# An opening list planned with other step lengths on TensorE, and idle matrix products placed only in that list's gaps

## The chip, the cores and the metric

One core of one Trainium2 chip. The metric is the device time of one execution in microseconds (us), lower is better; comparisons use the median of several executions.

## The reference

Attention in two parts over 8 batches, 8 heads, 576 positions and 64 dimensions, summed, and then a normalised gated feed-forward layer over the 4608 tokens. Cut to what matters:

```python
# coarse part: q, k, v averaged over groups of 4 positions, 144 x 144 softmax, repeated 4 times
out_up = np.repeat(sm_attn(q_d, k_d, v_d), 4, axis=2)
# local part: every position sees the positions at a distance under 4
mask = np.abs(pos[:, None] - pos[None, :]) < 4
scores = np.where(mask, 0.125 * np.matmul(q, k.transpose(0, 1, 3, 2)), -1e9)
out_local = np.matmul(softmax(scores), v)
x = (out_up + out_local)            # 4608 tokens x 512
xn = x / np.sqrt(np.mean(x * x, -1, keepdims=True) + 1e-6) * rms_g
g = xn @ w_gate                     # 512 -> 1536
return (g / (1 + np.exp(-g)) * (xn @ w_val)) @ w_out
```

The weights come as 64-bit numbers; the kernel takes two 32-bit words of each and makes a high and a low part of it.

## The kernel before, in words

The tokens are worked in 18 chunks of 256. For a chunk the local attention makes x, x is normalised and turned (`turn`, TensorE transposes into PSUM), split into `xh` (ScalarE) and `xl` (VectorE, line 304), and the feed-forward layer (`Forward`) runs over 12 slices f of the hidden width: `first` (two groups of 12 products into one `ps_h` buffer, gate and value), `tanh` on ScalarE, `gate` and `product` on VectorE, `high` (ScalarE) and `low` (VectorE or GpSimd), and `second`, 6 products into `ps_o`, two slices later.

The start of the program is different, and all of the change lies in it. It makes at once: the sums of q, k, v over groups of 4 (`OpeningSums`); eight coarse pieces p0 to p7, one for each pair of heads of the first two batches (`Coarse`: `scores`, `peak`, `powers`, `turn`, `copy`, `values`, `scaled`, `store`); the local attention of chunks 0, 1 and 2 on TensorE (`Dense`, which I call c0, c1 and c2: `scores`, softmax, `flip`, `copy`, `values`, then `add_up` of the pieces for c0 and `add_rows` for c1 and c2); the decoding of 36 blocks of weights (`load_weight`: `fetch` on the SP queue, `scale`, `last_bits`, `join`, `high`, `split` on ScalarE and VectorE); and `Forward` of chunk 0. Every one of these steps is a task with an engine, a length in us, a due time, the tasks it comes after and the buffers it takes. `Plan.run` goes through them as a list scheduler: of the steps that can start first, on the engine that can start first, the one with the earliest due time is written out next. So the lengths in the `task(...)` calls set the order of the instructions on each engine; they have no other effect. The order is then fixed, and an engine that comes to a step too early waits there. What follows (chunks 1 to 17 of `Forward`, with the attention of the chunk after) is written out in loops and ordered without these lengths.

TensorE's clock is granted by a gate, in steps that the profile shows. To keep it up, the kernel writes idle products: matrix products of a bf16 unit matrix into an accumulator that the next step overwrites anyway. Before the change these are in `place`, which every `Coarse` step that takes an accumulator calls: two products of 224 columns each time.

PSUM has three `ps_h`, two `ps_o` and three `ps_a` accumulators; pieces p0, p2, p4, p6 use `ps_a`, the others `ps_h`. The raw weight blocks have eight places until their `join` is done.

Of the kernel before, what the change touches and what calls it, by code (L numbers as in the profile page):

```python
# [19 lines left out]
P = 128  # L20
B, H, S, D = 8, 8, 576, 64
FAC = 4
SD = S // FAC
# [4 lines left out]
DM, DF = H * D, 1536  # L28
# [13 lines left out]
FIRST = 1  # L42
WARM = 2
V_ROWS = 50.0
# [31 lines left out]
class Plan:  # L76
# [33 lines left out]

    def start(self):
        free = self.free = {e: 0.0 for e in ("PE", "ACT", "DVE", "POOL", "SP", "DMA", "PORT")}
# [16 lines left out]
    def run(self, until=1e9):  # L129
        free, ready = self.free, self.ready  # L130
        while self.left:
# [18 lines left out]
            s, e, t = best  # L150
            if s >= until:
                return
            cost = next(o for o in t.options if o[0] == e)[1]
            t.start = s
            free[e] = s + cost - OVERLAP.get(e, 0.0)
            if t.port and e in SHARING:
# [20 lines left out]
def attn_moe_kernel(  # L177
# [280 lines left out]
    def sums_of(b, hp):  # L458
        if (b, hp // 2) not in sums:
            sums[b, hp // 2] = Sums(b, hp // 2)  # L460
        return sums[b, hp // 2]

    class Coarse:

# [31 lines left out]
        def plan(self, at, after=()):  # L496
# [16 lines left out]
            for par in range(2):  # L513
                turn = task("PE", 0.55, lambda par=par: self.turn(par), at - TAIL, [exps[par]], allocs=[t[par]], uses=[a[par]])
                copies.append(task("ACT", 0.38, lambda par=par: self.copy(par), at, [turn], uses=[a[par], t[par]]))
            inv = task("DVE", 0.33, self.invert, at, exps, uses=[z])
            values = self.valued = task("PE", 1.3, self.values, at - TAIL, [*copies, *sm.ready_vs], allocs=[o], uses=[*a, sm.vs_buf])
            scaled = self.done = task("DVE", 0.42, self.scaled, at, [values, inv], allocs=[og], uses=[o, z])
# [24 lines left out]
        def place(self, n=2 * SD):  # L543
            if loose:
                return self.pool.tile([HALF, n], FP32, name=self.tag)
            t = self.pool.tile([P, DM], FP32, name=self.tag)
            for _ in range(WARM):
                nc.tensor.matmul(
                    out=t[:, 2 * SD:].rearrange("p (t c) -> p t c", t=2), lhsT=masks["ident"],
                    rhs=bcast(masks["ident"][:, :(DM - 2 * SD) // 2], 1, 2), start=True, stop=True, skip_group_check=True,  # L550
                )
            return t[:HALF, :n]
# [319 lines left out]
    class Dense:  # L872
# [8 lines left out]
        def plan(self, sums, pieces, mask, at, end):  # L881
# [14 lines left out]
            for par in range(2):  # L896
                sb = s_bufs[par] if early else s_bufs[0]
                made = self.plan_softmax(par, at, scores, made, sp[par], sb)
                t = made[0]
                tp = buf("ps_a")  # L900
                t = task("PE", 0.7, lambda par=par: self.flip(par), at, [t], allocs=[tp], uses=[sb, tp])
# [14 lines left out]
            for par in range(2):  # L916
                values.append(task(
                    "PE", 0.8, lambda par=par: self.values(par), end - 15 + par,
                    [copies[par], *v_ready, *values[-1:], *(first if early else [p.valued for p in pieces])],
                    allocs=[] if early or par else x_bufs, uses=[*x_bufs, *v_bufs, *s_bufs],  # L920
                ))
# [8 lines left out]
            else:  # L930
                end += 25.0
                t = task(
                    "ACT", 0.1, self.load_up, end - 12, [stored[p.b, p.hp] for p in pieces], allocs=[self.xh_buf],
                    uses=[self.xh_buf], lag=9.0,
                )
                ups = [task("PE", 1.6, self.add_rows, end - 12, [t, *values], uses=[self.xh_buf, *x_bufs])]
            self.valued = values[-1:]
# [9 lines left out]
            for b in range(2):  # L947
                xs, tps = x_ts[b], buf("ps_h" if early else "ps_a")
                norms = self.plan_norms(b, xs, x_bufs, root, end)
                turn = task(  # L950
                    "PE", 0.6, lambda b=b: self.turn(b), end - 7 - TAIL, [*norms, *self.turns],
                    allocs=[tps] + ([self.xh_buf, self.xl_buf][not early:] if b == 0 else []), uses=[xs, self.xh_buf, self.xl_buf],
# [60 lines left out]
        def plan_scores(self, sums, pieces, mask, at, late):  # L1013
# [78 lines left out]
        def scores(self, b):  # L1092
            if b == 0:
                self.s = [ps_h.tile([P, 2, 2, 2, D], FP32, name="ps_h") for _ in range(2)]
                for par in range(2):
                    nc.tensor.matmul(
# [159 lines left out]
        def turn(self, b):  # L1256
# [5 lines left out]
            pool, tag = (ps_a, "ps_a") if self.c else (ps_h, "ps_h")  # L1262
            tp = self.xp[b] = pool.tile([P, KT, P], FP32, name=tag)
            for k in range(KT):
                last = nc.tensor.transpose(out=tp[:, k], in_=self.xn[b][:, k * P:(k + 1) * P], identity=ident_sb).ins
# [17 lines left out]
    class Forward:  # L1283
# [136 lines left out]
    def decode(n):  # L1420
# [9 lines left out]
        bits = task(  # L1430
            (("ACT", 0.67, at), ("DVE", 0.6, at)), 0, lambda e: last_bits(e.lower()), at, [got], uses=[raw],
        )
# [4 lines left out]
        joined.append(join_)  # L1437
        hi = task((("ACT", 0.62, at), ("DVE", 0.35, at)), 0, lambda e: high(e.lower()), at, [join_, *own], uses=[w])
        whole[n] = task("DVE", 0.69, split, at, [hi], uses=[w], port=True)
# [71 lines left out]
    with tc.manual_schedule():  # L1511
        plan.run()
    loose.append(True)
    listed.append(opened.copied)

# [97 lines left out]
```

## Time and profile before

| | |
|---|---|
| three executions | 1088.72, 1087.98, 1086.74 us (median 1087.98) |
| profiled execution | 1088.73 us, its span 1087.0 us, mean granted TensorE clock 0.983 |
| TensorE busy | 1044.5 us, 96% of the span |
| VectorE, ScalarE, GpSimd busy | 887.4, 626.4, 168.0 us |
| chain that ended last | TensorE 81%, VectorE 9%, DMA 4%, ScalarE 3% |

The span is the time from the first to the last instruction; the remaining 1.73 us of the profiled execution lie around it. Times in rows of the profile are us from the start of the span, a lone "x8" counts instructions, and the bracket at a row's end is the idle time of the engine ahead of it and what ended it. Steps are recorded one by one, so the step of a row is told by its line: 534 `scores`, 548 idle products, 574 `turn`, 589 `values` of a piece, 1096 and 1110 `scores` of a Dense chunk, 1158 `flip`, 1181 `values` of a Dense chunk, 1193 `add_up`, 1265 `turn` of a Dense chunk, 1344 `first`, 1380 `second`.

### The profile page before, as it was taken

What the parts mean: (1) busy time and instruction counts of PE and PEld (TensorE: products, weight loads), DVE (VectorE), ACT (ScalarE), POOL (GpSimd) and SP (SyncE); (2) the same over time, 40 slices, a digit from 0 to 9 for tenths busy, and PEclk for the clock granted to TensorE, in tenths of its full rate; (3) what the DMA queues carried; (4) which work ended last, traced back from release to release, by engine and by line L of the source; (5) the groups of instructions that cost most, each with busy time, mean ns of one, the idle gap of its engine ahead of it and who ended that gap; (6) DMA issues with size and microseconds to landing.
All of it is one profiled execution on the core that took longest, in us unless ns stands there. A gap on an engine that the chain in (4) does not pass through costs nothing.

```text
span 1087.0 us, 23815 instructions
## 1 busy us (share of the span) xinstructions
PE 1044.5 (96%) x8804; PEld 958.7 (88%) x8804; DVE 887.4 (82%) x1988; ACT 626.4 (58%) x2308; POOL 168.0 (15%) x225
## 2 busy tenths in 40 slices
PE   4888899899999999999999999999999999999998
PEld 2667799689998999999999999999999999999997
DVE  5778859885979998989898898989899998986432
ACT  5588743843747483848384838384738383746222
POOL 3201300312121121212121212020202010111000
PEclk8888999999999999999999999999999999999999
DMA  8488842564362635353535353313132222210000
GB/s 264 135 277 309 223 116 75 116 160 83 91 130 63 134 94 118 85 119 87 126 81 123 77 129 81 97 41 106 43 105 61 82 86 65 84 40 21 1 21 20
DMA packets 72731, 113.28 MB, mean 104 GB/s; under 512 B 26006, under 2 KB 33958, under 8 KB 72614
## 3 DMA queue, kind: packets, MB, share of 16 engines
q1 hardware_dynamic: 46342, 91.64, 27.7%
q0 software_dynamic: 8768, 15.95, 9.4%
q10 hardware_dynamic: 17504, 4.16, 1.8%
q8 instruction: 69, 1.13, 0.4%
q14 instruction: 48, 0.39, 0.1%
HBM read 99.92 MB, written 11.80 MB: 103 GB/s over the span
## 4 chain that ended last, share of the span: by engine, by line
PE 81%; DVE 9%; DMA 4%; ACT 3%; issue 2%; SPq 0%; ACTq 0%; POOL 0%; DVEq 0%; POOLq 0%
PE ps_h L1344 48%; PE ps_o L1380 25%; PE ps_a L589 2%; DVE prod L711 1%; PE ps_a L534 1%; PE ps_a L861 1%; DMA qk<-in_qk_sum_dram 1%; PE ps_a L574 1%; DVE sc L715 1%; ACT a_g L565 1%; DMA vs<-in_v_sum_dram 1%; DVE sil L1355 1%; DVE x_t L784 1%; DVE sil L1360 1%; DMA wo<-in_qk_sum_dram 1%
## 5 line engine op out<-in xcount | busy, mean ns | idle before, releaser
L1380 PE MATMUL ps_o<-wo,hs 128*128 128x512 f32 x1296 | 336.0, 397 | 0.9 <-DVE hs L1369 0.9
L1344 PE MATMUL ps_h<-xh,wg 128*128 128x256 f32 x1728 | 314.3, 279 | 0.0
L1344 PE MATMUL ps_h<-xh,wv 128*128 128x256 f32 x1728 | 310.0, 277 | 0.0
L1344 PEld LDWEIGHTS ps_h<-xh,wg 128*128 128x128 f32 x1728 | 267.1, 190 | 5.9 <-issue 0.4
L1344 PEld LDWEIGHTS ps_h<-xh,wv 128*128 128x128 f32 x1728 | 263.8, 188 | 3.4 <-issue 0.2
L1380 PEld LDWEIGHTS ps_o<-wo,hs 128*128 128x128 f32 x1296 | 228.9, 188 | 39.0 <-DVE hs L1369 1.1
L758 ACT ACTIVATE prod<-kv,sc 128x64 f32<-128x64 f32 x960 | 247.8, 427 | 16.0 <-DVE sc L749 11.3
L1344 PE MATMUL ps_h<-xl,wg 128*128 128x256 f32 x864 | 243.2, 282 | 7.8 <-DVE sil L1360 5.5
L1344 PE MATMUL ps_h<-xl,wv 128*128 128x256 f32 x864 | 241.5, 279 | 3.8 <-DVE sil L1355 3.8
L1352 ACT ACTIVATE sil<-ps_h 128x256 f32<-128x256 f32 x216 | 83.5, 387 | 224.7 <-PE ps_h L1344 205.8
L1344 PEld LDWEIGHTS ps_h<-xl,wg 128*128 128x128 f32 x864 | 163.8, 190 | 14.6 <-DVE sil L1360 6.6
L1344 PEld LDWEIGHTS ps_h<-xl,wv 128*128 128x128 f32 x864 | 162.4, 188 | 8.6 <-DVE sil L1355 4.8
L1366 ACT ACTIVATE hs<-sil 128x256 fp32r<-128x256 f32 x216 | 90.0, 418 | 132.4 <-DVE sil L1360 108.9
L765 POOL TENSOR_TENSOR prod<-sc,kv 128x256 f32<-128x256 f32 x120 | 92.3, 808 | 402.8 <-DVE sc L749 175.5
L784 DVE TENSOR_REDUCE x_t<-prod 128x128 f32<-128x896 f32 x120 | 127.4, 1073 | 20.9 <-PE ps_a L861 14.2
L1355 DVE SCALAR_TENSOR_TENSOR sil<-sil,ps_h 128x256 f32<-128x256 f32 x216 | 89.5, 414 | 61.6 <-ACT sil L1352 56.3
L711 DVE TENSOR_TENSOR prod<-q_t,kv 128x896 f32<-128x896 f32 x120 | 129.7, 1083 | 1.4 <-DMA kv<-in_k_pad_dram 1.2
L715 DVE TENSOR_REDUCE sc<-prod 128x14 f32<-128x896 f32 x120 | 128.2, 1075 | 0.0
L1369 DVE TENSOR_TENSOR hs<-sil,hs 128x256 fp32r<-128x256 f32 x213 | 93.4, 439 | 33.2 <-ACT hs L1366 33.1
L1360 DVE SCALAR_TENSOR_TENSOR sil<-sil,ps_h 128x256 f32<-128x256 f32 x216 | 89.3, 414 | 5.9 <-PE ps_h L1344 4.5
L372 POOL DMA_DIRECT2D qk<-in_qk_sum_dram x36 | 32.4, 900 | 253.4 <-DMA qk<-in_qk_sum_dram 222.2
L765 DVE TENSOR_TENSOR prod<-sc,kv 128x128 f32<-128x128 f32 x120 | 53.6, 467 | 0.7
(187 smaller groups left out, 940.8 us busy)
## 6 DMA issues: line engine op xcount, KB each, us to landing
kv<-in_k_pad_dram SPq DMA_DIRECT2D x60, 320.0 KB
kv<-in_v_pad_dram SPq DMA_DIRECT2D x60, 320.0 KB
qk<-in_qk_sum_dram POOLq DMA_DIRECT2D x36, 288.0 KB, 5.0
q_t<-in_q_band_dram SPq DMA_DIRECT2D x60, 128.0 KB
out_dram<-o_sb SPq DMA_DIRECT2D x30, 256.0 KB
vs<-in_v_sum_dram POOLq DMA_DIRECT2D x36, 144.0 KB, 3.4
qk<-in_qk_sum_dram SPq DMA_DIRECT2D x12, 288.0 KB
wo<-in_qk_sum_dram SPq DMA_DIRECT2D x2, 1152.0 KB
```

Source lines behind the costliest of these rows:

```text
L711: nc.vector.tensor_tensor(out=pr, in0=bcast(q[:, s0:s0 + 2], 2, NO), in1=window(k, s0), op=ALU.mult)
L715: nc.vector.tensor_reduce(out=self.sc[:, j, par, s0:s0 + 2], in_=self.pr[i], axis=AX.X, op=ALU.add,)
L758: nc.scalar.activation(out=self.pr[i][:, o, s], in_=self.v[j, par][:, s0 + s + o], func=AF.Copy, scale=p[:, s, o:o + 1],)
L765: (nc.vector if engine == "DVE" else nc.gpsimd).tensor_tensor(out=self.pr[i][:, a:b], in0=bcast(p[:, :, a:b].rearrange("p s o -> p o s"), ...
L784: nc.vector.tensor_reduce(out=self.x[j][:, s0:s0 + 2, par], in_=pr.rearrange("p o s d -> p s d o"), axis=AX.X, op=ALU.add,)
L1344: last = nc.tensor.matmul(out=self.p[f][:, t], lhsT=wi(f)[:, 0, k], rhs=xi[:, k], start=(n == 0), stop=(n == 3 * KT - 1),).ins
L1352: nc.scalar.activation(out=self.sil[f], in_=self.p[f][:, 0], func=AF.Tanh, scale=0.5)
L1355: nc.vector.scalar_tensor_tensor(out=self.sil[f], in0=self.sil[f], scalar=1.0, in1=self.p[f][:, 0], op0=ALU.add, op1=ALU.mult,)
L1360: nc.vector.scalar_tensor_tensor(out=self.sil[f], in0=self.sil[f], scalar=0.5, in1=self.p[f][:, 1], op0=ALU.mult, op1=ALU.mult,)
L1366: nc.scalar.activation(out=self.hs[f][:, 0], in_=self.sil[f], func=AF.Copy)
L1369: (nc.gpsimd if engine == "POOL" else nc.vector).tensor_tensor(out=self.hs[f][:, 1], in0=self.sil[f], in1=self.hs[f][:, 0], op=ALU.subtract,)
L1380: last = nc.tensor.matmul(out=self.o[j], lhsT=lhs[:, cols], rhs=rhs(f)[:, 0], start=(f == 0 and i == 0), stop=(f == NF - 1 and i == 2),).ins
```

## The change

The lengths of TensorE's steps in the opening are set to others (and three of VectorE's), so the list comes out in another order. The scheduler notes, for each TensorE step, how long it finds TensorE idle ahead of it (`plan.idle`). Idle products are no longer written at each `place`: a new function `warm` writes one for each 0.2 us of that noted idle time, at most 24, and it is called by every step that takes a new accumulator, `Dense.scores`, `flip`, `turn` and `first` included. The noted time goes to zero once used, and each later TensorE step overwrites it, so idle time ahead of a step that takes no accumulator is not filled. An idle product now has 256 columns. Two orderings are added (the load of the coarse rows for c1 after c0's `turn`, c2's `flip` after c1's `values`); for c2's load of coarse rows, c1's `turn` takes the place of the stores.

```diff
-WARM = 2
+IDLE = 0.2
+MOST = 24
...
             t.start = s
+            if e == "PE":
+                self.idle = s - free[e]
             free[e] = s + cost - OVERLAP.get(e, 0.0)
...
+    def warm(t):
+        n, plan.idle = min(int(plan.idle / IDLE), MOST), 0.0
+        for _ in range(n):
+            nc.tensor.matmul(
+                out=t[:, :2 * P].rearrange("p (t c) -> p t c", t=2), lhsT=masks["ident"],
+                rhs=bcast(masks["ident"], 1, 2), start=True, stop=True, skip_group_check=True,
+            )
...
-                turn = task("PE", 0.55, lambda par=par: self.turn(par), at - TAIL, [exps[par]], allocs=[t[par]], uses=[a[par]])
+                turn = task("PE", 0.45, lambda par=par: self.turn(par), at - TAIL, [exps[par]], allocs=[t[par]], uses=[a[par]])
...
             t = self.pool.tile([P, DM], FP32, name=self.tag)
-            for _ in range(WARM):
-                nc.tensor.matmul(
-                    out=t[:, 2 * SD:].rearrange("p (t c) -> p t c", t=2), lhsT=masks["ident"],
-                    rhs=bcast(masks["ident"][:, :(DM - 2 * SD) // 2], 1, 2), start=True, stop=True, skip_group_check=True,
-                )
+            warm(t)
...
-                    "ACT", 0.1, self.load_up, end - 12, [stored[p.b, p.hp] for p in pieces], allocs=[self.xh_buf],
+                    "ACT", 0.1, self.load_up, end - 12, [*[stored[p.b, p.hp] for p in pieces], *atts[0].turns], allocs=[self.xh_buf],
...
-                    "PE", 1.2 if b == 0 else 0.7, lambda b=b: self.scores(b), at + 2 * b,
+                    "PE", 2.2 if b == 0 else 1.15, lambda b=b: self.scores(b), at + 2 * b,
...
-                t = task("PE", 1.1, lambda par=par: self.flip(par), late + 8, made, allocs=[tp], uses=[sb, tp])
+                t = task("PE", 1.1, lambda par=par: self.flip(par), late + 8, [*made, *atts[1].valued], allocs=[tp], uses=[sb, tp])
...
-            task("ACT", 0.1, self.load_up, late + 20, [stored[p.b, p.hp] for p in pieces], allocs=[self.xh_buf], lag=9.0)
+            task("ACT", 0.1, self.load_up, late + 20, atts[1].turns, allocs=[self.xh_buf], lag=9.0)
...
             tp = ps_a.tile([P, 4, 2, D], FP32, name="ps_a")
+            warm(tp.rearrange("p x a k -> p (x a k)"))
...
                 self.p[f] = ps_h.tile([P, 2, C], FP32, name="ps_h")
+                warm(self.p[f].rearrange("p t n -> p (t n)"))
```

Of the other lengths: `values` of a piece 1.3 to 1.1, `flip` and `values` of a Dense chunk 0.7 and 0.8 to 1.1, `add_rows` 1.6 to 1.9, `turn` of a Dense chunk 0.6 to 0.8, `last_bits` on VectorE 0.6 to 0.42, `high` on VectorE 0.35 to 0.41.

The idle products, counted in TensorE's list: 80 of 224 columns before, two at each of 40 places. After, 24 ahead of p0's `scores`, 10 ahead of p0's `turn`, 10 ahead of p1's `turn`, 1 and 14 ahead of the `scores` of c0 and c1, none from there to p6's `values` (about 24 to 68 us of the old timeline), then 5 ahead of those, 1 ahead of c2's first `flip`, 18 and 1 ahead of c0's two `turn` steps, 15 ahead of the first `first`, and 5 ahead of the fifth: 104 of 256 columns.

Three places show what else moved. The first is the SP queue, between the loads of c0's rows (line 1049) and the first weight blocks (line 258); line 606 stores a piece's result. Before:

```order
L1049 DMA kv<-in_v_sum_dram 64x1x512 x3
L606 DMA up<-o_g 72x4x64
L1049 DMA kv<-in_v_sum_dram 64x1x512 x2
L258 DMA wg_1_702<-in_w_gate_dram 128x1024
L258 DMA wg_1_702<-in_w_val_dram 128x1024
L258 DMA wg_1_715<-in_w_out_dram 128x1024
L258 DMA wg_1_715<-in_w_gate_dram 128x1024
L606 DMA up<-o_g 72x4x64
```

and now, with the same steps on lines 1057, 262 and 614:

```order
L1057 DMA kv<-in_v_sum_dram 64x1x512 x5
L262 DMA wg_1_684<-in_w_gate_dram 128x1024
L262 DMA wg_1_684<-in_w_val_dram 128x1024
L262 DMA wg_1_712<-in_w_out_dram 128x1024
L614 DMA up<-o_g 72x4x64
L262 DMA wg_1_712<-in_w_gate_dram 128x1024
```

The first three weight blocks and the last two row loads no longer stand behind the store of p2's result.

The second is TensorE around the `scores` of p5 (`ps_h<-xh`), which are the first row before:

```order
L534 MATMUL ps_h<-xh 72x144 x4
L548 LDWEIGHTS q_t
L548 MATMUL ps_a<-q_t 128x224
L548 LDWEIGHTS q_t
L548 MATMUL ps_a<-q_t 128x224
L589 MATMUL ps_a<-hs,a_g 72x64 x8
L1181 MATMUL ps_o<-kv,x_t 32x64 x32
L1193 MATMUL ps_o<-o_g,q_t 32x128 x4
```

and the third row now, where 1168 is `flip`, 1203 `add_up`, 546 `scores`, 582 `turn`, 1191 `values` of c0 and 597 `values` of a piece:

```order
L1168 MATMUL ps_a<-ident_sb,wo_1_455 64x64 x16
L1203 MATMUL ps_o<-o_g,q_t 32x128 x4
L546 MATMUL ps_h<-xh 72x144 x4
L582 MATMUL ps_a<-ident_sb,a_g 72x72 x8
L1191 MATMUL ps_o<-kv,x_t 32x64 x32
L597 MATMUL ps_a<-hs,a_g 72x64 x8
L582 MATMUL ps_h<-ident_sb,a_g 72x72 x8
L1203 MATMUL ps_o<-o_g,q_t 32x128 x4
```

The idle products are gone, p5's `scores` stand ahead of p4's `turn`, and c1's second `flip` stands ahead of p5's `scores` (before, both of c1's `flip` steps came after the `scores` of p6).

The third is VectorE at the end of c0's attention, from the normalisation of x (line 1252) to `xl` (line 304). Before:

```order
L1252 TENSOR_SCALAR x_t<-ps_o,rinv 128x256 x2
L279 SCALAR_TENSOR_TENSOR o_sb<-o_sb,wg_1_715 128x512 x2
L279 SCALAR_TENSOR_TENSOR o_sb<-o_sb,wv_1_771 128x512
L294 TENSOR_TENSOR wv_0_876<-o_sb,wv_0_875 128x4x128
L304 SCALAR_TENSOR_TENSOR xl<-ps_h,g_sb,xh 128x128 x8
```

and now, the same steps on lines 1262, 283 (`join`), 298 (`split`), 295 (`high`) and 308:

```order
L1262 TENSOR_SCALAR x_t<-ps_o,rinv 128x256 x2
L283 SCALAR_TENSOR_TENSOR o_sb<-o_sb,wg_1_712 128x512
L283 SCALAR_TENSOR_TENSOR o_sb<-o_sb,wv_1_769 128x512 x2
L298 TENSOR_TENSOR wo_0_922<-o_sb,wo_0_921 128x512
L295 CAST wv_0_878<-o_sb 128x4x128
L308 SCALAR_TENSOR_TENSOR xl<-ps_h,g_sb,xh 128x128 x4
L298 TENSOR_TENSOR wg_0_820<-o_sb,wg_0_819 128x4x128
L308 SCALAR_TENSOR_TENSOR xl<-ps_h,g_sb,xh 128x128 x4
```

One more decoding step stands ahead of the first half of `xl`, and one between its halves. In ScalarE's list a `high` stands likewise between the halves of `xh`. Counted from the start to VectorE's first step of c0's normalisation, the list now holds 10 `join`, 10 `split` and 6 `last_bits` (before 10, 9 and 4); to ScalarE's first `squares`, 11 `scale`, 8 `high` and 5 `last_bits` (before 10, 7 and 6).

After the opening the instructions are the same, apart from buffer numbers; in the chunks that follow it at once some steps stand a few products earlier or later.

More of the change, by code (lines that the diff above doesn't have):

```diff
@@ L111, in start @@
     def start(self):
+        self.idle = 0.0
         free = self.free = {e: 0.0 for e in ("PE", "ACT", "DVE", "POOL", "SP", "DMA", "PORT")}
@@ L513, in plan @@
             for par in range(2):
-                turn = task("PE", 0.55, lambda par=par: self.turn(par), at - TAIL, [exps[par]], allocs=[t[par]], uses=[a[par]])
+                turn = task("PE", 0.45, lambda par=par: self.turn(par), at - TAIL, [exps[par]], allocs=[t[par]], uses=[a[par]])
                 copies.append(task("ACT", 0.38, lambda par=par: self.copy(par), at, [turn], uses=[a[par], t[par]]))
             inv = task("DVE", 0.33, self.invert, at, exps, uses=[z])
-            values = self.valued = task("PE", 1.3, self.values, at - TAIL, [*copies, *sm.ready_vs], allocs=[o], uses=[*a, sm.vs_buf])
+            values = self.valued = task("PE", 1.1, self.values, at - TAIL, [*copies, *sm.ready_vs], allocs=[o], uses=[*a, sm.vs_buf])
             scaled = self.done = task("DVE", 0.42, self.scaled, at, [values, inv], allocs=[og], uses=[o, z])
@@ L900, in plan @@
                 tp = buf("ps_a")
-                t = task("PE", 0.7, lambda par=par: self.flip(par), at, [t], allocs=[tp], uses=[sb, tp])
+                t = task("PE", 1.1, lambda par=par: self.flip(par), at, [t], allocs=[tp], uses=[sb, tp])
                 t = task(
@@ L917, in plan @@
                 values.append(task(
-                    "PE", 0.8, lambda par=par: self.values(par), end - 15 + par,
+                    "PE", 1.1, lambda par=par: self.values(par), end - 15 + par,
                     [copies[par], *v_ready, *values[-1:], *(first if early else [p.valued for p in pieces])],
@@ L932, in plan @@
                 t = task(
-                    "ACT", 0.1, self.load_up, end - 12, [stored[p.b, p.hp] for p in pieces], allocs=[self.xh_buf],
+                    "ACT", 0.1, self.load_up, end - 12, [*[stored[p.b, p.hp] for p in pieces], *atts[0].turns], allocs=[self.xh_buf],
                     uses=[self.xh_buf], lag=9.0,
                 )
-                ups = [task("PE", 1.6, self.add_rows, end - 12, [t, *values], uses=[self.xh_buf, *x_bufs])]
+                ups = [task("PE", 1.9, self.add_rows, end - 12, [t, *values], uses=[self.xh_buf, *x_bufs])]
             self.valued = values[-1:]
@@ L950, in plan @@
                 turn = task(
-                    "PE", 0.6, lambda b=b: self.turn(b), end - 7 - TAIL, [*norms, *self.turns],
+                    "PE", 0.8, lambda b=b: self.turn(b), end - 7 - TAIL, [*norms, *self.turns],
                     allocs=[tps] + ([self.xh_buf, self.xl_buf][not early:] if b == 0 else []), uses=[xs, self.xh_buf, self.xl_buf],
@@ L1094, in scores @@
                 self.s = [ps_h.tile([P, 2, 2, 2, D], FP32, name="ps_h") for _ in range(2)]
+                warm(self.s[0].rearrange("p b t a k -> p (b t a k)"))
                 for par in range(2):
@@ L1263, in turn @@
             tp = self.xp[b] = pool.tile([P, KT, P], FP32, name=tag)
+            warm(tp.rearrange("p k n -> p (k n)"))
             for k in range(KT):
@@ L1430, in decode @@
         bits = task(
-            (("ACT", 0.67, at), ("DVE", 0.6, at)), 0, lambda e: last_bits(e.lower()), at, [got], uses=[raw],
+            (("ACT", 0.67, at), ("DVE", 0.42, at)), 0, lambda e: last_bits(e.lower()), at, [got], uses=[raw],
         )
@@ L1437, in decode @@
         joined.append(join_)
-        hi = task((("ACT", 0.62, at), ("DVE", 0.35, at)), 0, lambda e: high(e.lower()), at, [join_, *own], uses=[w])
+        hi = task((("ACT", 0.62, at), ("DVE", 0.41, at)), 0, lambda e: high(e.lower()), at, [join_, *own], uses=[w])
         whole[n] = task("DVE", 0.69, split, at, [hi], uses=[w], port=True)
@@ L1513, in attn_moe_kernel @@
     loose.append(True)
+    plan.idle = 0.0
     listed.append(opened.copied)
```

## Prediction

> **What bounds the kernel now.** I read the slices first, then a table of stretches, then the chain that ended last, and behind each piece of the chain its row in the timeline.
>
> The page's slices (27.2 us each; tenths of busy time, and the granted TensorE clock in tenths):
>
> ```profile
> PE   4888899899999999999999999999999999999998
> PEclk8888999999999999999999999999999999999999
> ```
>
> From the sixth slice on TensorE is at nine tenths or more; the room is in the first five. The stretches (us; then busy time of PE, PEld, DVE, ACT, POOL with their instructions; granted clock, DMA share, GB/s):
>
> ```profile
> 0.00:86.50 86.50, 59.61 (x1214) 45.58 (x1214) 63.01 (x154) 56.02 (x170) 14.46 (x30) 0.83 0.73 234
> 86.50:156.00 69.50, 64.75 (x569) 58.44 (x569) 52.85 (x122) 49.19 (x109) 12.90 (x15) 0.97 0.72 204
> 500.00:700.00 200.00, 200.00 (x1575) 185.73 (x1575) 182.09 (x393) 122.39 (x494) 36.59 (x46) 1.00 0.42 103
> ```
>
> Up to the first `first` product at 86.5 us TensorE idles 86.50 - 59.61 = 26.9 us at a clock of 0.83; in the next 69.5 us it idles 4.75; later nothing. What the feed-forward part does after that is the same work on a full TensorE, so a microsecond by which the opening ends sooner is a microsecond of the time, unless decoding makes TensorE wait again.
>
> The clock decides inside the opening. The same table in steps of the gate (about 3.41 us); then, in the same columns up to PEld, the idle products alone; then the wait before the gate shut:
>
> ```profile
> 43.33:46.74 3.41, 2.48 (x35) 1.77 (x34) 2.88 (x10) 2.18 (x9) 0.56 (x1) 1.00 0.23 56
> 46.74:50.16 3.42, 2.23 (x30) 1.82 (x28) 3.35 (x10) 1.59 (x7) 2.34 (x4) 0.99 0.84 261
> 50.15:60.40 10.25, 9.57 (x124) 7.19 (x124) 7.34 (x20) 7.15 (x23) 0.00 (x0) 0.50 0.80 283
> 53.57:56.99 3.42, 3.42 (x26) 2.77 (x25) 1.96 (x4) 1.43 (x3) 0.00 (x0) 0.50 0.97 355
> 60.40:77.60 17.20, 16.81 (x424) 13.89 (x422) 14.77 (x36) 15.98 (x46) 0.00 (x0) 1.00 0.90 284
> 91.14:94.56 3.42, 1.92 (x17) 1.72 (x15) 1.38 (x4) 1.81 (x4) 0.00 (x0) 1.00 0.93 346
> ```
>
> ```profile
> 43.33:60.40 17.07, 4.62 (x24) 2.17 (x24) 0.70 0.70 233
> 60.40:77.60 17.20, 4.04 (x24) 1.52 (x22) 1.00 0.90 284
> ```
>
> ```profile
> 50.24 0.69 PE L574 MATMUL ps_a<-ident_sb,a_g 72*72 72x72 f32 x4 [1.27 <-ACT a_g L565]
> ```
>
> After a step 73% busy (2.48 of 3.41) the clock stayed; after one 65% busy (2.23 of 3.42) it went to 0.50 and stayed there for three steps, one of them (53.57) without a pause. Yet `first` kept it with 56% (1.92 of 3.42) at 91.14. So the busy share alone doesn't tell; what runs counts too.
>
> **The change, term by term.** The sum is made against the profiled execution, 1088.73 us (span 1087.0 and 1.73 around it). The median of the runs shown is 0.75 below it, and I take that off at the end.
>
> *Start to 43 us: 0.* Fewer products stand here, some on the chain, but both lists have the same real steps in nearly the same order, and what ends the stretch is VectorE's and ScalarE's work. What may change it is this piece of the chain, inside c1's `scores`:
>
> ```profile
> 25.16 3.42 issue
> ```
>
> TensorE waits for nothing that the profile shows there. With other instruction counts ahead of it this pause falls elsewhere, some 80 instructions later, where the same `scores` still bound. Ends: -1.0 (two pairs of products that leave the chain, each by the 0.48 of such a pair in the chain below) and +0.7 (an estimate: a fifth of the pause coming on top of the wait that it falls into).
>
> *43 to 60.6 us: -4.8.* The chain before, all of it TensorE at half clock:
>
> ```profile
> 52.38 0.66 PE ps_o L1193 x8
> 53.03 0.86 PE ps_h L548 x4
> 53.89 1.17 PE ps_h L534 x8
> 55.06 0.48 PE ps_a L548 x2
> 55.55 1.91 PE ps_a L589 x16
> 57.45 1.86 PE ps_o L1181 x64
> 59.31 0.58 PE ps_o L1193 x8
> 59.90 0.73 PE ps_a L548 x4
> ```
>
> and the same steps at full clock, from the chain (the first three) and the timeline:
>
> ```profile
> 34.05 1.03 PE ps_h L589 x16
> 35.08 0.36 PE ps_o L1193 x8
> 35.92 0.65 PE ps_a L534 x8
> 62.20 1.10 PE L1181 MATMUL ps_o<-kv,x_t 64*32 64x64 f32 x64
> ```
>
> Before: 0.66 + 0.86 + 1.17 + 0.48 + 1.91 + 1.86 + 0.58 + 0.73 = 8.25. Without products and at full clock: 0.36 + 0.65 + 1.03 + 1.03 (a little less than the 1.10, since neighbours overlap) + 0.36 = 3.43. So -4.8. If the gate shuts as before, only the products go: 0.86 + 0.48 + 0.73 = 2.07. These are the ends.
>
> What is late next is the decoding on ScalarE and VectorE; it must start as much sooner, or it takes the place of the chain. On the SP queue and in ScalarE's first decoding step before:
>
> ```profile
> 44.85 0.32 SPq L606 DMA_DIRECT2D up<-o_g  x1
> 45.22 1.30 SPq L1049 DMA_DIRECT2D kv<-in_v_sum_dram  x2
> 46.56 0.59 SPq L258 DMA_DIRECT2D wg<-in_w_gate_dram  x1
> ```
>
> ```profile
> 52.84 1.22 ACT L262 ACTIVATE o_sb<-wg 128x512 f32<-128x512 f32 x2
> ```
>
> The first fetch is issued at 46.56 because p2's store, which waits for its result until 44.85, stands ahead of it. Now three fetches and two row loads stand ahead of the store. They can go as soon as the ten row loads are out, about 42, so 4 to 5 us sooner, and the first `scale` at about 48. The store itself slips behind three fetches, some 1.5 us; its reader is c1's load of coarse rows, which now waits until c0's `turn`, long after. That later load (and c2's, now behind c1's `turn`) feeds `add_rows`, which before stood well behind c0's `first`; I cost it at nothing, with that as its cover.
>
> *60.6 to 77 us: -0.6.* Here the chain runs over ScalarE, and the copies of c1's two `flip` steps were on it:
>
> ```profile
> 67.44 0.48 ACT wo L1169
> 72.05 0.59 ACT wo L1169
> ```
>
> The flips now come before p5's `scores` and p6's, so 0.48 + 0.59 = 1.07 leave this stretch; one decoding piece more ahead of `squares` gives back about 0.5. Ends -1.6 and 0.
>
> *`squares` to the first `first`: +0.4.* Rows of c0's `turn` at half clock, of a later one at full clock (from the chain), and of a `split` on VectorE:
>
> ```profile
> 82.44 1.94 PE L1265 MATMUL ps_h<-ident_sb,x_t 128*128 128x128 f32 x8 [4.82 <-DVE x_t L1252]
> 185.43 0.94 PE ps_a L1265 x8
> 84.40 0.69 DVE L294 TENSOR_TENSOR wv<-o_sb,wv 128x512 fp32r<-128x512 f32 x1
> ```
>
> 18 products ahead of `turn` keep TensorE busy for some of the 4.82 us of idling, so `turn` may run in 0.94 instead of 1.94; half of that hides behind VectorE's decoding: -0.5. On VectorE a `high` (estimated at half a split) now stands ahead of `xl` and a `split` between its halves: 0.69 + 0.35, less an overlap of 0.1, is +0.9. Ends -0.5 and +1.4. The products themselves end before the last normalised half arrives even at half clock (four of 224 columns took 0.86 in the chain above; 18 of 256 would take 4.4 us, in 4.82).
>
> *First `first`: -1.4.* Its 24 products at half clock and the same number at full clock:
>
> ```profile
> 86.55 5.12 PE ps_h L1344 x24
> 135.50 3.10 PE ps_h L1344 x24
> ```
>
> The 15 products ahead of it fill the wait for `xl`, which was idle before, so the gate should open: 3.10 - 5.12 = -2.0. Two splits then stand on VectorE between the first `gate` and the next; +0.6. Ends -2.0 and 0.
>
> *The rest of `Forward` of chunk 0, and chunk 1: +1.0.* Waits such as this one,
>
> ```profile
> 94.58 0.38 PE L1344 MATMUL ps_h<-xl,wv 128*128 128x256 f32 x1 [1.52 <-DVE sil L1355]
> ```
>
> come where TensorE reaches a product before VectorE's `gate`, which queues behind decoding. The weights come sooner by what the opening gains, so they should not grow by much; five products ahead of the fifth `first` (0.55) and a few value products that chunk 1 now lists ahead of its first `tanh` (0.5) cost. Ends -3 (below, as a rival) and +2.5.
>
> Sum: 0 - 4.8 - 0.6 + 0.4 - 1.4 + 1.0 = -5.4, so 1083.3 for the profiled execution and 1082.6 for the median.
>
> **Rivals.** *The gate shuts once, as before.* Without its products the stretch from 43.33 to 60.40 holds 2.48 + 2.23 + 9.57 - 4.62 = 9.66 us of real work in 17.07, much of that at half clock; c1's flips come in, but I get no more than 65 to 70% for a step at full clock, about what the step had after which the gate shut. Then the second term is -2.07 and the sum -2.7: 1085.3.
>
> The Trainium skill ("TensorE: Matmul & The Clock Gate", section "HAM oscillation — how this bites in real kernels") lets the clock fall only for idle gaps over about 3.4 us. By that rule the gate would stay open from 43 to 77 us, and the sum would be the -5.4. The trace disagrees: the gate shut at 50.15 behind a longest gap of 1.27 us. The measurement decides, so this rival keeps a large chance.
>
> *Slower: the gate shuts a second time, between 60 and 77 us.* Real work there was 16.81 - 4.04 = 12.77 of 17.20, 74%, next to the 73% that held. Three steps of half clock (10.25 us, as long as the shut stretch before) would turn 7.6 us of work into 15.2: 5.0 us if all of it lies on the chain, half that if ScalarE's decoding hides half; 3.7 taken. `turn` and the first `first` then stay cold too (the -0.5 and the -1.4 fall away). -2.7 + 3.7 + 1.9 = +2.9: 1090.9. From a cost of 0.8 us in that stretch on, the change is slower than before. Against it: the chain there was ScalarE's, so TensorE has some slack.
>
> The same page's section "A second HAM failure mode: psum-queue depth-cycling" reports short idle times between groups that make the clock swing, which is this mechanism; the shut step at 50.15 agrees with it.
>
> *More: decoding that starts sooner also takes the waits from chunk 0's `Forward`.* TensorE idles 4.75 us there; two thirds of it gone is -3.1, while the last term's products stay: -5.4 - 3.1 = -8.5, 1079.5 (its +1.0 is those products).
>
> *No gain: decoding is the bound.* Both decoders are nearly full ahead of c0's normalisation:
>
> ```profile
> 70.00:80.00 10.00, 7.23 (x224) 5.64 (x220) 9.15 (x28) 10.00 (x31) 0.00 (x0) 1.00 0.96 318
> ```
>
> VectorE 9.15, ScalarE 10.00 of 10, and the DMA share 0.96. If the fetches, not their order, set the pace, what TensorE saves comes back as a wait for weights: about 1087. Against it: from 43 to 60 us ScalarE had 6 us idle (2.18 + 1.59 + 7.15 busy of 17.07), which earlier fetches can fill.
>
> **How the numbers follow.** Forecast 0.36 (own range 1081 to 1084.5), gate shut once 0.26, second shutting 0.19, decoding bound 0.11, more 0.08. A change of 0.2%, 2.2 us, is about what a measurement can tell from none. Faster: 0.36 + 0.08 and 0.16 of the gate's 0.26, in all 0.60. Slower: 0.14 of the second shutting's 0.19 and 0.02 of the decoding's, 0.16. The same: the other 0.24. Range 1079 to 1090: it leaves out half of the gain rival and most of the slow one, near 0.17.
>
> **What would show it.** The granted clock after 33 us: 1.00 up to 77 us by the forecast, one stretch at 0.50 by the first rival, two by the second. The first `scale` at about 48 us, c0's `squares` about 70 instead of 77.08, the first `first` at about 80 and in near 3.1 us. c1's flip copies off ScalarE's chain. TensorE's idle time from the first `first` to 156 us: near 5 us by the forecast, under 2 if the gain rival holds, and over 8 if decoding bounds. The prediction is wrong if the first `first` starts sooner and the end does not, or if p4 to p7 run at half clock.

## The result and the profile after

The changed kernel takes 1094.02 us in the median (1088.36 to 1100.20) against 1087.98, a ratio of 1.0061 with a 95% interval of 1.0038 to 1.0084: slower, by 0.61% or 6.6 us (6.0 between the medians), where 1082.6 was forecast. Its profiled execution takes 1093.37 us, with a span of 1091.6. Disturbed runs are left out of all ratios here.

The slices of the page after, to be held against those of the prediction:

```profile
PE   5988998699999999999999999999999999999998
PEclk9789999799999999999999999999999999999999
```

The eighth slice, 191 to 218 us, is new: TensorE six tenths busy at a clock of 0.7, where it was at eight tenths and 0.9 before. That lies in chunk 1, behind everything that the change edits. So the span is best cut where `Forward` of chunk 1 begins (its first `tanh`) and where chunk 4's begins. Before, in the columns of the stretch tables (TensorE's busy time is the third number, the granted clock the third from the end):

```profile
0.00:150.56 150.56, 118.92 (x1652) 99.81 (x1656) 114.59 (x272) 102.87 (x271) 27.36 (x45) 0.89 0.74 226
150.56:340.64 190.08, 183.04 (x1524) 166.07 (x1517) 151.89 (x341) 102.86 (x404) 36.83 (x47) 0.99 0.46 106
```

and after:

```profile
0.00:146.48 146.48, 124.20 (x1676) 103.44 (x1680) 114.18 (x273) 100.94 (x270) 28.34 (x45) 0.91 0.77 233
146.48:344.66 198.18, 185.62 (x1524) 169.03 (x1517) 149.32 (x341) 103.15 (x403) 37.48 (x47) 0.97 0.44 102
```

The opening with chunk 0 ends 4.08 us sooner. Chunks 1 to 3 then take 198.18 instead of 190.08 us, 8.10 more, for the same 1524 TensorE instructions. Of these, 12.56 - 7.04 = 5.52 us are more idle time of TensorE, and the other 2.58 are more busy time, at a mean clock of 0.97 instead of 0.99. After chunk 4's first `tanh` another 0.62 is lost. The gain is there; it is lost twice over in code that the change does not name.

The waits behind the 5.52, as rows of TensorE in the changed kernel (in brackets the idle time ahead of the row and what ended it; 1356 is `first`, 1372 `product`):

```profile
168.81 0.39 PE L1356 MATMUL ps_h<-xl,wg 128*128 128x256 f32 x1 [1.03 <-DVE sil L1372]
194.37 0.58 PE L1356 MATMUL ps_h<-xl,wg 128*128 128x256 f32 x1 [5.64 <-DVE sil L1372]
216.60 0.58 PE L1356 MATMUL ps_h<-xl,wg 128*128 128x256 f32 x1 [5.38 <-DVE sil L1372]
```

The middle one stood in the kernel before too (4.93 us, up to 197.17, and behind it 3.4 us at half clock). The other two are new. Now each long wait is followed by 6.8 us at half clock, the second time with TensorE busy for 3.79 of them only:

```profile
193.10:199.90 6.80, 5.53 (x27) 5.51 (x28) 5.88 (x15) 6.80 (x33) 2.61 (x4) 0.50 0.44 95
213.60:220.40 6.80, 3.79 (x17) 3.80 (x18) 6.80 (x13) 2.42 (x13) 1.68 (x2) 0.50 0.56 134
```

What VectorE does while TensorE waits for the third (719 and 723 are `score` and its sum, of chunk 4's attention; 568 is `scale` of a coarse piece; 1367 `gate`, 1381 `low`, 1372 `product`):

```profile
212.42 1.08 DVE L719 TENSOR_TENSOR prod<-q_t,kv 128x896 f32<-128x896 f32 x1
213.42 0.41 DVE L1367 SCALAR_TENSOR_TENSOR sil<-sil,ps_h 128x256 f32<-128x256 f32 x1
213.75 1.07 DVE L723 TENSOR_REDUCE sc<-prod 128x14 f32<-128x896 f32 x1
214.75 0.41 DVE L1381 TENSOR_TENSOR hs<-sil,hs 128x256 fp32r<-128x256 f32 x1
215.08 0.16 DVE L568 TENSOR_SCALAR m_g<-m_g 72x4 f32<-72x4 f32 x1
215.15 1.07 DVE L723 TENSOR_REDUCE sc<-prod 128x14 f32<-128x896 f32 x1
216.14 0.41 DVE L1372 SCALAR_TENSOR_TENSOR sil<-sil,ps_h 128x256 f32<-128x256 f32 x1
```

and the same steps before (560 `scale`, 1355 `gate`, 715 the sum, 1360 `product`):

```profile
211.40 0.15 DVE L560 TENSOR_SCALAR m_g<-m_g 72x4 f32<-72x4 f32 x1
...
212.46 0.41 DVE L1355 SCALAR_TENSOR_TENSOR sil<-sil,ps_h 128x256 f32<-128x256 f32 x1
212.79 1.07 DVE L715 TENSOR_REDUCE sc<-prod 128x14 f32<-128x896 f32 x1
...
215.72 0.41 DVE L1360 SCALAR_TENSOR_TENSOR sil<-sil,ps_h 128x256 f32<-128x256 f32 x1
```

Before, `scale` stood ahead of the attention's first sum; now it stands behind two of its sums (the first of them at 207.42) and comes 3.7 us later, although chunk 1 began 4.08 us sooner. And TensorE's list has changed too: the piece's `turn` and a `second` stood in the gap, at 213.18 and 213.68, and now stand behind the waiting `first`:

```profile
213.18 0.70 PE L574 MATMUL ps_a<-ident_sb,a_g 72*72 72x72 f32 x8 [0.27 <-ACT a_g L565]
213.68 1.63 PE L1380 MATMUL ps_o<-wo,hs 128*128 128x512 f32 x6
```

```profile
220.89 0.67 PE L582 MATMUL ps_a<-ident_sb,a_g 72*72 72x72 f32 x8
221.36 1.63 PE L1392 MATMUL ps_o<-wo,hs 128*128 128x512 f32 x6
```

Why the order moved is read from the source. The opening stands in `with tc.manual_schedule()`, but the kernel as a whole is built under `TileContext(nc, schedule_with_timeline_sim=True)`: what follows the opening is ordered by a timeline that the framework simulates while it builds. That this timeline begins with the opening, so that the lengths reach the order behind it after all, is the likely link; no run turned it off. What is certain is that the order moved: counted in the two orders that e5 and e6 below write out, another instruction stands at 333 places of TensorE's list, 158 of VectorE's and 129 of ScalarE's, all of them ahead of chunk 4.

### The profile page after: what moved, and what is told of

It is laid out like the page before. It is cut to its first block, busy times and chain, and to the rows that moved or that the text cites. A ratio compares the mean times of both kernels' runs of the same rounds, so it can differ in the third digit from the quotient of the medians.

```text
span 1091.6 us, 23871 instructions
## 1 busy us (share of the span) xinstructions
PE 1053.0 (96%) x8828; PEld 965.6 (88%) x8828; DVE 886.7 (81%) x1989; ACT 624.2 (57%) x2307; POOL 168.8 (15%) x225
## 4 chain that ended last, share of the span: by engine, by line
PE 84%; DVE 5%; ACT 4%; DMA 3%; issue 2%; SPq 1%; POOL 0%; ACTq 0%; POOLq 0%; DVEq 0%
PE ps_h L1356 50%; PE ps_o L1392 26%; PE ps_a L597 2%; PE ps_a L546 1%; PE ps_a L869 1%; PE ps_a L582 1%; DVE prod L719 1%; DMA wo<-in_qk_sum_dram 1%; ACT a_g L573 1%; DMA qk<-in_qk_sum_dram 1%; ACT prod L766 1%; SPq L1057 1%; DVE sc L723 1%; ACT o_sb L266 1%; DMA wg<-in_w_val_dram 1%
```

## The experiments

The kernel before ran again beside each of four groups of runs, with medians of 1087.79 (e1 to e4), 1087.36 (e5 to e8), 1089.20 (e9 to e12) and 1087.15 us (e13). "Opening" is the time to chunk 1's first `tanh`, "chunks 1 to 3" the time from there to chunk 4's, "idle" TensorE's in the latter; all three of the one profiled execution.

| kernel | opening, order after it | median us | ratio, 95% | opening | chunks 1 to 3 | idle |
|---|---|---|---|---|---|---|
| before | old, old | 1087.98 | 1 | 150.56 | 190.08 | 7.04 |
| e1 | old without idle products, old | 1086.04 | 0.9972 [0.9950, 0.9994] | 150.37 | 189.19 | 6.71 |
| e7 | old, old replayed | 1087.92 | 1.0009 [0.9989, 1.0029] | 150.85 | 188.49 | 6.22 |
| e5 | new, old replayed | 1083.24 | 0.9963 [0.9942, 0.9984] | 145.78 | 190.36 | 7.20 |
| e8 | new with two idle products a step, old replayed | 1082.28 | 0.9951 [0.9933, 0.9970] | 144.36 | 189.18 | 5.77 |
| e12 | new without idle products, old replayed | 1083.60 | 0.9954 [0.9928, 0.9981] | 148.54 | 188.27 | 5.56 |
| after | new, new | 1094.02 | 1.0061 [1.0038, 1.0084] | 146.48 | 198.18 | 12.56 |
| e2 | new, 21 more idle products; new | 1093.52 | 1.0052 [1.0029, 1.0074] | 147.69 | 201.42 | 15.14 |
| e3 | new, new with two holds | 1095.58 | 1.0068 [1.0044, 1.0092] | 149.12 | 198.03 | 13.31 |
| e4 | new without those at `first`, new | 1101.62 | 1.0102 [1.0067, 1.0137] | 153.59 | 199.65 | 14.83 |
| e6 | old, new replayed | 1098.43 | 1.0110 [1.0084, 1.0136] | 149.09 | 198.34 | 12.34 |
| e9 | new, mixed | 1094.35 | 1.0057 [1.0033, 1.0082] | 145.19 | 197.65 | 12.15 |
| e10 | new, mixed | 1097.13 | 1.0088 [1.0059, 1.0117] | 144.97 | 202.62 | 16.37 |
| e11 | new, mixed | 1100.92 | 1.0117 [1.0077, 1.0158] | 151.38 | 208.21 | 17.38 |
| e13 | new, mixed | 1096.90 | 1.0089 [1.0061, 1.0117] | 146.62 | 201.85 | 14.18 |

The column "chunks 1 to 3" is the finding at a glance: 188 to 190 us wherever the old order stands, 198 to 208 wherever it does not.

**e1: the old opening without idle products.**

```diff
-WARM = 2
+WARM = 0
```

> The kernel before without any of its 80 idle products; the lists of all engines after the opening are the same as before, word for word. Theory 1 (the loss of the changed kernel comes from the order that the program's scheduler gives the instructions of chunks 1 and 2, which depends on the opening): with the order unchanged, whatever the opening gains or loses shows in full at the end: if the gate behaves as before, the products' 2.1 us on the chain and some more before go, 1084 to 1086 us; chunk 1's first tanh moves by the same amount as the end. Theory 2 (whatever makes the opening end sooner is lost in chunk 1, since VectorE's attention of chunk 2 sets the time there): the end does not move though chunk 1's first tanh does, 1088. Theory 3 (the prediction's slow rival, products needed for the clock): the gate shuts more often, chunk 1's first tanh comes later, 1090 or more.

It was slightly faster, by 0.28%, at the edge of what theory 1 gave. The 80 idle products of the kernel before were worth nothing or less; the profiled opening is only 0.2 us shorter, so the profile doesn't show where the gain lies.

**e2: 36 products ahead of the first `first` instead of 15.**

```diff
-                warm(self.p[f].rearrange("p t n -> p (t n)"))
+                for n in ((20, 16) if self.c == 0 and f == 0 else (None,)):
+                    plan.idle = plan.idle if n is None else n * IDLE + 0.01
+                    warm(self.p[f].rearrange("p t n -> p (t n)"))
```

> The changed kernel with 36 in place of 15 idle products ahead of the first `first` product, which only delays the opening's end; the lists after the opening are those of the changed kernel. Theory 1 (order): the delay of about 2.2 us (21 times 0.107) goes through to the end, 1096 us. Theory 2 (the opening came too soon for chunk 2's attention): the stalls in chunk 1 shrink by the delay and the time stays, 1094 us, or falls.

The time is the one that theory 2 gave, but not for its reason: the waits did not shrink. TensorE idles 15.14 us in chunks 1 to 3 instead of 12.56, and the wait of 5.38 us is 6.92 here. Theory 1's 1096 was missed as well, so this run does not tell the two apart.

**e3: two steps of TensorE's list put back.** `first` of (2,1) and (2,3), chunk and slice, is held behind `second` of (1,7) and (1,8).

```diff
+    HELD = {(2, 1): (1, 7), (2, 3): (1, 8)}
...
-            last = fwd.emit(f)
+            with behind(done2.get(HELD.get((c, f)))):
+                last = fwd.emit(f)
...
-                    last = fw.emit_second(g)
+                    last = done2[fw.c, g] = fw.emit_second(g)
```

> The changed kernel, where chunk 2's second and fourth groups of `first` products are held behind chunk 1's `second` of slices 7 and 8, so that TensorE again does a piece's `turn`, a `second`, the next piece's `scores`, `values` and a `second` ahead of them, as before the change. The opening is untouched. Theory 1 (order on TensorE): the 5.4 us stall at 211 us goes, and the shut gate behind it (about 1.9 us): 1086 to 1088 us. Theory 2 (VectorE's attention sets the time there): the stall moves to the next accumulator, 1093 to 1095 us.

The wait moved to the piece's `turn`, whose operand now comes too late from `scale` by way of ScalarE:

```profile
220.14 1.17 PE L582 MATMUL ps_a<-ident_sb,a_g 72*72 72x72 f32 x8 [5.92 <-ACT a_g L573]
```

Theory 1's time, 1086 to 1088, was missed: these two holds on TensorE alone do not undo the loss.

**e4: no idle products at `first`.** The call of `warm` in `first` is removed.

> The changed kernel without the 20 idle products ahead of the first and fifth `first`; all other instructions and all lists after the opening are as in the changed kernel. By the prediction's term for the first `first` (half clock without the products) chunk 1's first tanh comes 1.4 us later less the 0.55 of the five; by the order theory the end moves with it: 1094 to 1096 us. If the products there do nothing for the clock: 1093 to 1094 us.

Both expectations were missed, by 5 us and more. The opening of the profiled execution is 7 us longer. In it the gate was shut for 37.5 us from 44.4 us on, which begins ahead of everything that this edit touches. Seven of the eight executions took 1097.06 to 1103.69 us, one 1088.93; why so many were long stays open. Chunks 1 to 3 lose as much as in the changed kernel.

**e5 to e8: opening and order taken apart.** In these kernels nothing after the opening is left to the framework's scheduler. Each step there is stopped ahead of every instruction, and all 10844 instructions are written out in a given order, which is read off the built list of the one or the other kernel:

```diff
+        with tc.manual_schedule():
+            for k in ORDER:
+                i = owner[k]
+                r = started(i)
+                while at[i] <= k:
+                    r.go()
+                    at[i] += 1
```

e5 is the new opening with the old order, e6 the old opening with the new order, and e7, the control, the old opening with the old order. e8 is e5 with at least two idle products at each piece's step that takes an accumulator (176 in all):

```diff
+            plan.idle = max(plan.idle, 2 * IDLE + 0.01)
             warm(t)
```

> The opening of the changed kernel, and after it all engines' lists written out by hand in the order that they have in the kernel before (same instructions, only their order from chunk 1 on). Theory 1 (order): the 8 to 11 us that the changed kernel and its variants lose between chunk 1's and chunk 4's first tanh are not lost, chunk 4's first tanh comes at most 1 us later relative to chunk 1's than before, and the opening's lead is kept: 1082 to 1087 us. Theory 2 (the sooner opening itself collides with chunk 2's attention): the 8 us are lost with any order, 1092 to 1096 us.

> The reverse: the opening of the kernel before, and after it all engines' lists in the order of the changed kernel. Theory 1 (order): it loses 8 to 11 us between chunk 1's and chunk 4's first tanh, although its opening is untouched: 1095 to 1098 us. Theory 2 (collision): 1087 to 1089 us.

> Opening and order of the kernel before, the order written out by hand as in the two runs beside it, to see what writing it out does by itself. All theories: 1088 us, the time of the kernel before.

> As the first run of these four (new opening, old order), but every step that takes an accumulator of a piece writes at least two idle products (72 more than the change's 104). If the change's opening loses time because the gate shuts where the products went (the prediction's rivals), the clock after 33 us stays up for longer, chunk 1's first tanh comes 1 to 3 us sooner than in the first run of these four, and the time is as much lower. If products only take time on TensorE: 1 to 3 us slower.

The control is not to be told from the kernel before, so writing the old order out costs nothing that these runs can tell; the new opening with the new order written out was not run. e5 came out as theory 1 said, and e6 at the upper end of it. The two stretches of e5, then of e6:

```profile
0.00:145.78 145.78, 124.04 (x1676) 104.03 (x1680) 114.09 (x273) 101.36 (x270) 28.40 (x45) 0.91 0.77 234
145.78:336.14 190.36, 183.16 (x1524) 166.52 (x1517) 149.98 (x341) 102.71 (x403) 37.15 (x47) 0.98 0.46 106
```

```profile
0.00:149.09 149.09, 118.38 (x1652) 100.17 (x1656) 114.78 (x272) 103.00 (x271) 27.62 (x45) 0.92 0.75 228
149.09:347.43 198.34, 186.00 (x1525) 169.49 (x1518) 150.45 (x342) 103.35 (x404) 37.55 (x47) 0.97 0.44 102
```

The loss goes with the order and not with the opening: e6 has the old opening and the wait of the changed kernel,

```profile
219.36 0.58 PE L1473 MATMUL ps_h<-xl,wg 128*128 128x256 f32 x1 [5.43 <-DVE sil L1489]
```

By medians the order costs 1098.43 - 1087.92 = 10.5 us with the old opening and, by the ratios of after and e5, 0.98% or 10.7 us with the new one. The opening is worth 1083.24 - 1087.92 = -4.7 us with the old order and, by the ratios of after and e6, -0.49% or -5.3 us with the new one. e8 beats both kernels: 0.9951 of before, though its interval overlaps with those of e5 and e12. Its gate stayed open from 30.0 to 190.4 us and its opening is 1.4 us shorter than e5's, as the expectation had it.

**e9 to e12: which part of the order, and what the idle products do.** All have the new opening. In e9, 139 instructions of chunk 4's attention (none on TensorE) are taken back to their old places in the new order; in e10 they are brought forward to their new places in the old order; e11 has the old list on TensorE and the new one on every other engine. e12 is e5 with `MOST = 0`, so no idle product is written.

> New opening; everything after it in the order that the changed kernel has, TensorE's list included, except that the 139 steps of chunk 4's attention (on VectorE, ScalarE, GpSimd and SyncE, none on TensorE) stand where the old order has them, so that VectorE makes chunk 1's last two gates ahead of that attention's scores. Theory V (VectorE's list: the next attention was pulled ahead of the gates): the 5.4 us wait near 211 us is gone or under 2 us, and the time is 1083 to 1087. Theory P (TensorE's list: a whole `first` ahead of the third piece's `turn` and of `second`): it stays at 1091 to 1096.

> New opening; everything after it in the old order, TensorE's list included, except that chunk 4's attention stands as early as the changed kernel's order has it. Theory V: VectorE reaches the last gates of chunk 1 later, TensorE waits 4 to 6 us near 208 to 215 us, and the time is 1088 to 1095. Theory P: TensorE's list is the old one, so it stays at 1082 to 1086.

> New opening; after it, TensorE's list is that of the old order and the lists of all other engines are the changed kernel's. Theory P: 1082 to 1086, as with the old order throughout. Theory V: the VectorE list still brings the gates late; 1090 to 1096, the wait of about 5 us between 205 and 216 us stays.

> New opening list without any idle product, old order after it. If the idle products hold the clock as the step with two of them at every piece suggested (1082.3 against 1083.2), without any the gate shuts for longer between 26 and 86 us and the time is 1085 to 1089. If the gain of the opening is its list alone, 1082 to 1085.

e9 took the wait of 5.38 us away, as the theory of VectorE's list said, but not the time. TensorE still idles 12.15 us there, in smaller waits behind VectorE:

```profile
168.25 0.38 PE L1484 MATMUL ps_h<-xl,wg 128*128 128x256 f32 x1 [1.37 <-DVE sil L1500]
211.60 0.38 PE L1484 MATMUL ps_h<-xl,wg 128*128 128x256 f32 x1 [0.71 <-DVE sil L1500]
224.88 0.38 PE L1484 MATMUL ps_h<-xl,wg 128*128 128x256 f32 x1 [1.71 <-DVE sil L1500]
283.13 1.21 PE L1520 MATMUL ps_o<-wo,hs 128*128 128x512 f32 x4 [1.72 <-DVE hs L1509]
```

e10 shows that the early attention is enough to lose: with the old TensorE list the pieces' `turn` steps now wait,

```profile
212.12 0.70 PE L754 MATMUL ps_a<-ident_sb,a_g 72*72 72x72 f32 x8 [4.04 <-ACT a_g L745]
230.25 1.06 PE L754 MATMUL ps_a<-ident_sb,a_g 72*72 72x72 f32 x7 [5.75 <-ACT a_g L745]
```

and e11 that the old TensorE list alone mends nothing. e11 took 1100.92 us, above the range of either theory, with a wait of 6.01 us at a `turn`. Neither theory gave the time of e9 and e10 both. e12 answers the other question: without any idle product the time is not to be told from e5's, so the 104 products are not what the new opening gains by. How much of the 4.7 us is its list is less clear than that: e1, the old list without its idle products, had 0.28% already. Held against e1, e12 is 0.9954 / 0.9972, some 2 us faster, and the two intervals overlap.

**e13: the last mixture.** TensorE's list and the attention as in the old order, only the steps of `Forward` and `Coarse` on the other engines as in the new one.

> New opening; after it TensorE's list and the place of chunk 4's attention are those of the old order, and only the steps of `Forward` and `Coarse` on VectorE, ScalarE, GpSimd and SyncE stand as in the changed kernel. Theory A (the place of the attention on VectorE decides, and TensorE's list has to go with it): 1082 to 1086, as with the old order throughout, no wait over 2 us between 200 and 235 us. Theory B (any mixture of the two orders loses, since each engine's list fits only the other lists of its own order): 1090 to 1100, with a wait of 4 us or more there.

Theory B's time: this mixture loses too. The wait at the `turn` fell to 1.70 us, below the 4 us that B named, and others took its place. All four mixtures lose about as much as the whole new order or more. As far as these four go, each engine's list fits only the others of its own order. What in the new order starts the loss was not narrowed further, and the new TensorE list with the old lists of all other engines was not run.

## Why the prediction was wrong

**The step that failed** is the sentence that "a microsecond by which the opening ends sooner is a microsecond of the time". It rested on stretches up to 156 us and on 500 to 700, where TensorE is full, and on "later nothing" for its idle time. Between them, in chunks 1 to 3, TensorE had 7.04 us of idle time, one wait of it 4.93 us behind VectorE's `product`; that stretch is not in the prediction. And the list there was taken as given, but for "some steps a few products earlier or later". That other order costs 10.5 us with an unchanged opening (e6), where the prediction put it at nothing. No rival named it, so the time fell outside the range of 1079 to 1090. The prediction's own sign came true: the first `first` started 2.78 us sooner (83.77 instead of 86.55), and the end came later.

**The sum for the opening** was right in sign and near in size: -5.4 was forecast; the profile after shows -4.08, the medians -4.7 and -5.3. Part of that nearness is luck. Three terms came out 1.55, 0.67 and 0.9 us worse than forecast, and the last one 1.8 better; and the openings of two executions of one list differ by more than such a term (last section). By its terms:

- *Up to c0's last `squares`, forecast 0 - 4.8 - 0.6 = -5.4, measured -3.85:*

```profile
78.03 0.41 ACT L1222 ACTIVATE x_t<-ps_o 128x256 f32<-128x256 f32 x1
```

```profile
74.18 0.38 ACT L1232 ACTIVATE x_t<-ps_o 128x256 f32<-128x256 f32 x1
```

  The first fetch of weights went out 2.4 us sooner, not 4 to 5, since the twelve row loads ahead of it, themselves behind a store at 35.37, were out only at 44.1:

```profile
44.14 0.59 SPq L262 DMA_DIRECT2D wg<-in_w_gate_dram  x1
```

  The miss lies in the first term, "start to 43 us: 0". The changed kernel reaches p2's `values`, 1.45 us later, though both lists have the same real steps ahead of it, but for one `add_up` that now stands behind. Before, and then now (the first row is of the chain, the others are of the timeline):

```profile
42.75 1.20 PE L589 MATMUL ps_a<-vs,a_g 72*72 72x64 f32 x16
```

```profile
20.89 2.40 PE ps_h L470 x14
44.20 1.25 PE L597 MATMUL ps_a<-vs,a_g 72*72 72x64 f32 x16
```

  "Fewer products stand here" is wrong: 59 idle products stand ahead of this place now, where 34 did, and 14 of them (line 470) are on the chain for 2.40 us. The gate was also shut from 25.9 to 39.5 us, where it had opened again at 33.1; no run separates the two. From there to the last `squares` the change gains 3.85 + 1.45 = 5.30 us, near the 4.8 + 0.6 of the forecast.

- *The gate.* It held from 39.5 to 66.8 us, where it had shut at 50.15; so the first rival, "the gate shuts once, as before", did not come true in this execution. In the six other profiles of the same list the gate shut sooner, at 42.4 (e3), 44.4 (e11), 56.0 (e10), 56.4 (e9), 56.9 (e5) and 57.7 us (e13), so there that rival's closing did come. In this one it shut later, as the second rival had it, between 60 and 77 us, behind a step 63% busy (2.15 of 3.40), but for two steps and not three:

```profile
39.50:66.80 27.30, 23.40 (x560) 18.41 (x560) 24.98 (x68) 24.20 (x81) 4.73 (x6) 1.00 0.90 291
63.40:66.80 3.40, 2.15 (x27) 1.73 (x26) 3.40 (x9) 3.40 (x13) 0.00 (x0) 1.00 1.05 329
66.80:73.60 6.80, 6.61 (x116) 5.03 (x119) 5.86 (x14) 5.57 (x16) 0.00 (x0) 0.50 0.83 285
```

  What this closing costs, no run shows.

- *`squares` to the first `first`: +0.4 forecast, (83.77 - 74.18) - (86.55 - 78.03) = +1.07 measured*, inside its ends. *First `first`: -1.4 forecast*, but the gate shut from 83.9 to 87.3 all the same, behind a step in which TensorE was busy for 1.23 of 3.41 us: the 15 products ended 2.18 us before `xl` came. Where the 24 products end, before (they start at 86.55) and after, is the start of the next one (`wv`):

```profile
91.49 0.28 PE L1344 MATMUL ps_h<-xl,wv 128*128 128x256 f32 x1
```

```profile
83.77 0.50 PE L1356 MATMUL ps_h<-xl,wg 128*128 128x256 f32 x1 [2.18 <-DVE xl L308]
...
88.22 0.28 PE L1356 MATMUL ps_h<-xl,wv 128*128 128x256 f32 x1
```

  They took 88.22 - 83.77 = 4.45 instead of 91.49 - 86.55 = 4.94, so -0.49. *The rest up to chunk 1: +1.0 forecast, (146.48 - 88.22) - (150.56 - 91.49) = -0.81 measured.* From the first `first` to 156 us, the stretch that the prediction named as a sign, TensorE idles 3.12 us instead of 4.71: fewer waits, the direction of the "more" rival.

**The other rivals.** "Decoding is the bound" is refuted by e5, which keeps the opening's gain to the end, and by the 3.12 us of idle time, where that rival had over 8. The slower rival found the right side by a wrong mechanism, which is luck: what cost the time lies over 110 us behind the place that it named.

## What to carry to other kernels

When a scheduler orders the code behind a hand-ordered part by a simulated timeline, an edit of that part can be two changes. Compare the built lists behind the edit as closely as those inside it, and before crediting a gain try the edit with the old order written out. Here, with TensorE and VectorE both nearly full, the lists were tuned as a set: moving one engine's list, or one part of a list, lost as much as moving all.

## What the runs showed of the hardware

One opening, instruction for instruction, took from 144.97 (e10) to 151.38 us (e11) to chunk 1's first `tanh`. The length goes with the time that the gate was shut ahead of that `tanh`: 23.8 us in e9 and e10 (145.19 and 144.97 us), 23.9 in e13 (146.62), 27.3 in the changed kernel and e5 (146.48 and 145.78), 40.9 in e3 (149.12) and 51.1 in e11. In e10 it was shut for 6.8 us from 56.0 on, in e11 for 27.4 us from 44.4 on, with TensorE fully busy all the time.

```profile
56.00:62.80 6.80, 6.80 (x110) 5.38 (x112) 5.39 (x13) 6.23 (x19) 0.00 (x0) 0.50 1.01 267
```

```profile
44.40:71.80 27.40, 27.40 (x358) 22.26 (x357) 19.21 (x53) 19.98 (x62) 2.00 (x4) 0.50 0.84 272
```

The boundaries of the steps lie at other moments of the program in these executions. The Trainium skill ("TensorE: Matmul & The Clock Gate", section "What's actually happening") says that the window is free-running and not reset by the kernel's start, which agrees with that. The same section of the Trainium skill says that one busy window of about 3.4 us brings the full clock back; the trace of e11 disagrees, where eight windows in a row, busy by the profile, did not. A single profile of an opening therefore tells its length to some 6 us only, and idle products placed by one such profile (104 in e5, 176 in e8, none in e12) made no difference that the medians can tell. They do hold the clock: the mean granted clock of e8's seven executions was 0.991 to 0.995, that of e12's 0.975 to 0.991.

The pause of TensorE in c1's `scores` goes with the instruction count, as the prediction says. In fourteen of the fifteen profiles TensorE stands still for 2 to 5 us behind its first 449 recorded products and weight loads, whichever step that is (3.42 us at 25.16 before, 3.73 at 23.30 after); in e2 it does so 256 records later, for 4.54 us. Since more idle products stand ahead of it now, it falls 88 records sooner among the `scores`, not later.
